# First product of the expert layer: float32r pairs become float16 pairs, and local heads are loaded in runs of six tokens

## The chip, the cores and the metric

The kernel runs on one core of a Trainium2 chip. The metric is the device time of one launch in microseconds (us). The kernel before took 700.45 us, the median of three runs (696.98 to 703.68). The engines are named as in the profile: PE (matrix products), PEld (PE's weight loads), DVE and ACT (vector and scalar engine), POOL (GpSimd) and SP, whose queue issues every DMA.

## The reference

Three layers follow each other. There are 4 batches of 576 tokens, 8 heads of 64 columns, and 2304 tokens of 512 columns in all.

```python
scores = q @ k.T / 8;  mask: heads 0-3 local (0 <= i-j < 32), heads 4-7 strided (j <= i, i % 32 == j % 32)
attn = softmax(where(mask, scores, -1e9));  x = attn @ v          # laid out as 2304 x 512
h = x @ w_in                                                      # 512 x 1024, the "first product"
sm = softmax(h);  solu = h * sm
ln = (solu - mean) / sqrt(var + 1e-6) * g_ln;  x = ln @ w_out     # 1024 x 512
a = x @ w_a;  b = x @ w_b;  out = (a * b) @ w_out2                # 512 x 1536 twice, 1536 x 512
```

q, k and v are float32; the weights arrive as float64 and are turned into float32 on the chip.

## The kernel before

**Order.** Every piece of work is recorded with `P.op` (engine, function, what it reads and writes); `Plan.schedule` (L243) then emits the pieces in the order of the list of numbers `ISSUE`. Each engine runs its own instructions strictly in that order, and the SP queue issues its DMAs in it too. Semaphores for the data and for the reuse of buffers follow from it.

**Attention.** A batch has four groups of two heads, two strided and then two local. `load_qk` (L549) loads q and k of a group; a strided group takes one DMA each, a local one takes a DMA per head and tensor, with 96 tokens on the partitions and runs of one token (64 floats). PE transposes them (L608), ACT copies the result out (L615, L618). Per tile, PE makes masked scores (L696, L701); DVE takes the row maximum (L719), subtracts it (L728), sums (L732) and inverts; ACT does the exponential (L731); POOL multiplies by the inverse (L768 or L777). Then there are two ways. A *direct* group (all of batch 0) is transposed in float32 by PE (L764), copied by ACT (L774) and multiplied with raw v in float32 (L798). Any other group is split: ACT writes a float16 copy of the weights (L784), POOL the rest (L785), the SP queue transposes the pair by DMA (L786), and v is a scaled float16 pair too (L644 on ACT, L647 on DVE), so that PE runs three float16 products (L803 to L805). The scale of v comes from `pair_scale` (L624), one for each two groups: a DVE maximum per group (L630), and a chain of small steps between PE and DVE (`pow2_scale`, L500 to L516). ACT writes the result to `xT` (L825).

**First layer.** `moe1` works on 18 tiles of 128 tokens. ACT rounds `xT` to float32r (`xh`, L845), DVE makes the rest (`xl`, L849). PE adds three passes (xh by the high weights, xh by the low weights, xl by the high weights), each of 4 products of 512 columns for each half of `h`, 24 in all (L856). `h` has one buffer: the next tile's products wait until DVE has taken the row maximum (L861), POOL has made a factor of it (L867 to L869) and DVE has multiplied `h` with the exponential (L871). ACT and DVE then make a float16 pair of the centred result (L875, L876), a DMA transposes it, and PE multiplies it with `w_out` in 48 products of 256 columns for each tile (L910).

**Weights of the first product.** `load_win` (L482) handles eight blocks of 128 x 512: SP loads the float64 words, ACT (L455) and DVE (L461, L465) make float32, ACT rounds to float32r (L474) and POOL subtracts (L475). A block's high half is ready as soon as it has been converted. `w_out` follows in the same way, but as a float16 pair with one scale for all (L492, L524, L526).

**Second layer.** From about 288 us on, float16 products of 384 and 256 columns (L1326, L1472) fill PE to the end.

## Time and profile before

| | |
|---|---|
| median of 3 runs | 700.45 us (696.98 to 703.68) |
| the profiled execution | 695.03 us, its span 693.3 us |
| busy: PE, DVE, ACT, POOL | 664.4, 571.5, 447.2, 144.7 us |
| idle of PE within the span | 28.9 us |

The profiled execution has 1.73 us around its span, and lies 5.42 us under the median. Engine rows count an instruction from its start to its end; neighbours on one engine overlap a little, so that a sum of means is some per cent above the busy time. A window of the profile gives the busy time of each engine in a stretch, and the rows of the timeline give the start of each instruction in us from the start of the span.

### The profile page before, as it was taken

The numbers are of one execution on the slowest core, as the hardware profiler recorded it, in microseconds if no ns is written. First come the engines' busy times: TensorE is split into PE (matmuls) and PEld (weight loads), VectorE is DVE, ScalarE is ACT, GpSimd is POOL, SyncE is SP. The second block draws the span as 40 slices with busy tenths as digits, with TensorE's granted clock in tenths as the row PEclk, the third lists the DMA queues.
The fourth block names the chain that finished last, engine by engine and source line by source line (L and its number), as shares of the span: only waits on it lengthen the run. The fifth ranks groups of instructions, "written<-read, shape, count | busy, mean of one in ns | idle before, by whom it ended". The sixth has DMA issues, their size and how long they took to land.

```text
span 693.3 us, 15572 instructions
## 1 busy us (share of the span) xinstructions
PE 664.4 (96%) x5991; PEld 498.8 (72%) x5991; DVE 571.5 (82%) x1238; ACT 447.2 (65%) x898; POOL 144.7 (21%) x268
## 2 busy tenths in 40 slices
PE   5987899999999999999999999999999999999997
PEld 4766677878787888886576676766767676775676
DVE  5789899789678644999999999799977989786576
ACT  3679868777767644986978787676543746434421
POOL 5544546536537432410000000000000000000000
PEclk9999899999999999999999999999999999999999
DMA  9999979999998434677254043653522304641023
GB/s 209 258 243 244 188 138 194 264 186 268 222 248 199 102 81 102 188 249 240 103 184 152 0 141 104 198 201 97 175 100 94 120 32 166 237 138 46 1 92 122
DMA packets 152650, 109.68 MB, mean 158 GB/s; under 512 B 101376, under 2 KB 131072, under 8 KB 152576
## 3 DMA queue, kind: packets, MB, share of 16 engines
q1 hardware_dynamic: 152576, 108.69, 60.4%
q8 instruction: 47, 0.77, 0.5%
q14 instruction: 27, 0.22, 0.1%
HBM read 65.41 MB, written 27.53 MB: 134 GB/s over the span
## 4 chain that ended last, share of the span: by engine, by line
PE 61%; DVE 8%; ACT 5%; issue 1%; POOL 0%; ACTq 0%; POOLq 0%
PE N L1326 17%; PE M L1326 13%; PE N L1472 9%; PE y L910 7%; PE M L1472 7%; PE h L856 6%; ACT y L1267 1%; DVE p L1423 1%; ACT w L1128 1%; DVE w L1132 1%; DVE y L1269 1%; DVE A L1415 1%; DVE A L1393 1%; DVE V L647 0%; ACT Z L1238 0%
## 5 line engine op out<-in xcount | busy, mean ns | idle before, releaser
L1326 PEld LDWEIGHTS <-w 128*128 128x128 f16 x1512 | 147.9, 98 | 91.7 <-issue 2.0
L1326 PE MATMUL N<-y,w 128*128 128x384 f16 x864 | 156.2, 326 | 0.7 <-ACT N L1333 0.7
L1472 PEld LDWEIGHTS <-p 128*128 128x128 f16 x1071 | 104.7, 98 | 20.4 <-issue 1.1
L1326 PE MATMUL M<-y,w 128*128 128x384 f16 x648 | 118.5, 326 | 0.8 <-ACT N L1333 0.8
L910 PE MATMUL y<-lnT,wout 128*128 128x256 f16 x864 | 101.4, 273 | 1.5 <-DMA lnT<-ln 0.8
L910 PEld LDWEIGHTS <-wout 128*128 128x128 f16 x864 | 82.0, 98 | 15.2 <-issue 4.1
L1418 ACT CAST p<-A 128x384 f16<-128x384 f32 x119 | 59.2, 512 | 40.1 <-DVE A L1393 22.6
L856 PE MATMUL h<-win,xh 128*128 128x512 f32 x288 | 79.8, 417 | 2.7 <-DVE wk L871 2.6
L1472 PE MATMUL N<-wo,p 128*128 128x256 f16 x612 | 77.7, 273 | 1.0 <-DVE yst L1488 1.0
L856 PEld LDWEIGHTS h<-win,xh 128*128 128x128 f32 x288 | 54.4, 198 | 14.4 <-DVE wk L871 3.3
L1423 DVE TENSOR_TENSOR p<-A,p 128x384 f16<-128x384 f32 x119 | 62.3, 552 | 2.7 <-ACT p L1418 2.7
L1472 PE MATMUL M<-wo,p 128*128 128x256 f16 x459 | 60.2, 273 | 0.0
L455 ACT ACTIVATE f64f<-raw 128x512 f32<-128x512 f32 x52 | 34.6, 674 | 11.2 <-DMA raw<-in_moe_w_in_dram 7.3
L856 PE MATMUL h<-win,xl 128*128 128x512 f32 x144 | 39.2, 394 | 0.0
L1415 DVE TENSOR_TENSOR A<-A 128x384 f32<-128x384 f32 x72 | 39.0, 553 | 0.2
L1488 DVE SCALAR_TENSOR_TENSOR ob<-M,osc,ob 128x256 f32<-128x256 f32 x63 | 27.8, 477 | 12.6 <-PE M L1472 11.1
L777 POOL TENSOR_TENSOR e<-e,r 128x324 f32<-128x324 f32 (+2 forms) x30 | 26.2, 881 | 50.0 <-DVE r L738 28.2
L861 DVE TENSOR_REDUCE st<-h 128x1 f32<-128x1024 f32 x18 | 22.0, 1220 | 17.2 <-PE h L856 17.1
L856 PEld LDWEIGHTS h<-win,xl 128*128 128x128 f32 x144 | 26.7, 188 | 5.9
L465 DVE SCALAR_TENSOR_TENSOR f64f<-f64f,raw 128x512 int32<-128x512 int32 x36 | 28.8, 804 | 2.3 <-ACT f64f L455 1.8
L1348 ACT COPY V<-M 128x384 f32<-128x384 f32 x36 | 17.0, 473 | 20.0 <-PE M L1326 19.9
L871 DVE SCALAR_TENSOR_TENSOR wk<-h,st,wk 128x1024 f32<-128x1024 f32 x18 | 23.0, 1279 | 7.8 <-POOL st L869 7.7
(191 smaller groups left out, 1207.0 us busy)
## 6 DMA issues: line engine op xcount, KB each, us to landing
raw<-in_moe_w_out_dram SPq DMA_DIRECT2D x20, 512.0 KB
o_scr<-ob SPq DMA_DIRECT2D x36, 256.0 KB
ob<-o_scr SPq DMA_DIRECT2D x30, 256.0 KB
raw<-in_moe_w_a_dram SPq DMA_DIRECT2D x12, 512.0 KB
raw<-in_moe_w_b_dram SPq DMA_DIRECT2D x12, 512.0 KB
y_scr<-y SPq DMA_DIRECT2D x14, 384.0 KB
y<-y_scr SPq DMA_DIRECT2D x14, 384.0 KB
y_scr<-ys SPq DMA_DIRECT2D x18, 256.0 KB
```

What stands on the lines that cost most here:

```text
L455: act(0.67, lambda: nc.scalar.activation(f(), raw()[:, :, 1].bitcast(F32), AF.Prelu, scale=2.0 ** -112, alpha=-2.0 ** 32), (raw,), (f,))
L465: dve(0.77, lambda: nc.vector.scalar_tensor_tensor(g().bitcast(I32), f().bitcast(I32), 3, raw()[:, :, 0], op0=ALU.logical_shift_left, op1= ...
L777: pool(0.1 + 1.2 * pl, lambda: nc.gpsimd.tensor_tensor(ev(), ev(), r()[:, :ng].unsqueeze(2).to_broadcast([128, ng, nk]), op=ALU.mult), (r, ...
L856: nc.tensor.matmul(h()[:, 512 * n:512 * n + 512], xs[xa]()[:, kk], win[wa][:, kk, 512 * n:512 * n + 512], start=(pi == 0 and kk == 0), sto ...
L871: dve(1.3, lambda: nc.vector.scalar_tensor_tensor(e(), h(), st()[:, 7:8], e(), op0=ALU.mult, op1=ALU.mult, accum_out=st()[:, 2:3]), (h, (s ...
L910: nc.tensor.matmul(y()[:, 256 * mi:256 * mi + 256], wout[:, kk, wa, 128 * m:128 * m + 128], lnT()[:, xa, kk], start=(pi == 0 and kk == 0), ...
L1326: nc.tensor.matmul(to()[:, :HB], w()[:, wa, a, kk], y7[b]()[:, xa, kk], start=first and pi == 0 and kk == 0, stop=pi == 2 and kk == 1, ski ...
L1415: dve(TD, lambda: nc.vector.tensor_tensor(to(), x(), y(), op=op), toks, (to,))
L1418: act(0.5, lambda: nc.scalar.copy(pu(0, a), x()), (x,), (pu.tok(0, a),))
L1423: dve(TD, lambda: nc.vector.tensor_tensor(pu(1, a), x(), pu(0, a), op=ALU.subtract), (x, pu.tok(0, a)), (pu.tok(1, a),))
L1472: nc.tensor.matmul(bk(i), pus[u](xa, a)[:, 128 * tt:128 * tt + 128], wo()[:, u, b, wa], start=a == A11 and u == 0 and pi == 0, stop=u == U ...
L1488: dve(0.475, lambda: nc.vector.scalar_tensor_tensor(dst(), bk(i), s(), dst(), op0=ALU.mult, op1=ALU.add), (src, osc), (obt(t, c),))
```

## The change

Four things change together.

1. `w_in` becomes a float16 pair. The eight blocks are converted to float32 (without rounding), ACT takes a sum of absolute values of each (L482 of the new file), one scale is made for all eight (`scale_win`), and only then are the pairs written: the high half by ACT (L489), the low half by DVE (L491, before on POOL). `xh` and `xl` are float16. The row maximum gets a small multiplication on DVE (L895), and POOL one more on its factor (L905), since `h` is now scaled.
2. v has one scale for each batch instead of each pair of groups (`batch_scale`), also in batch 0. `xT` stays scaled, and `unscale` holds the factor that takes both scales back.
3. The local groups of batch 0 are no longer direct: they are split like those of the later batches.
4. q and k of a local group come in one DMA each, with six neighbouring tokens on a partition (runs of 384 floats); POOL brings them into the former layout (L607).

```diff
-PARAM = dict(back=12, first=40, early=(0,), seed=4, noise=0.1, direct=((0, 0), (0, 1)), stay=0.0, pf1=(),
+PARAM = dict(back=12, first=40, early=(0,), seed=4, noise=0.1, direct=((0, 0),), stay=0.0, pf1=(),
-             PT=3, raw=2, rawl=2, raws=2, qkT=2, V=2, wk=2, xt=1, ln=2, lnT=2, ys=2, raw64=3, f64f=4, att=100.0,
+             PT=3, rawx=2, raw=2, rawl=4, raws=2, qkT=2, V=2, wk=2, xt=1, ln=2, lnT=2, ys=2, raw64=3, f64f=4, att=100.0,
...
 ISSUE = [int(n) for n in """
-10 0 13 11 14 5 2 15 16 1 12 6 18 17 21 8 35 19 9 20 7 4 22 414 37 430 3 771 787 36 39 38 40 43 41 42 181 187 23 66 44
...
-    win = [winp.tile([128, 4, FF1], F32R, name=f"win{i}") for i in range(2)]
+    win = winp.tile([128, 9, 2, DM], F16, name="win")
...
-        ring("win", tag, [128, 4, 128], F32R, pm["xt"])
+        ring("win", tag, [128, 4, 128], F16, pm["xt"])
...
-        split(f, lambda: win[0][:, kk, w], lambda: win[1][:, kk, w], ("win", kk, n), ph=i in pm["ph1"])
+        f = from_f64(w_in[128 * kk:128 * kk + 128, 1024 * n:1024 * n + 1024], False, fo, (("wif", c),))
+        act(0.78, lambda: nc.scalar.activation(f(), fo, AF.Abs, accum_out=wim[:, c:c + 1]), (("wif", c),), (f, ("wim", c)))
+    def scale_win():
+        pow2_scale(lambda: wim, [("wim", c) for c in range(8)], 8, 2, lambda: wisc, "wisc")
+    def split_win(c):
+        fo = win_f32(c)
+        act(0.71, lambda: nc.scalar.activation(win[:, c, 0], fo, AF.Copy, scale=wisc[:, 0:1]),
+            (("wif", c), "wisc"), (("wif", c - 1), ("win", c, 0)))
+        dve(0.85, lambda: nc.vector.scalar_tensor_tensor(win[:, c, 1], fo, wisc[:, 0:1], win[:, c, 0],
+                                                         op0=ALU.mult, op1=ALU.subtract),
+            (("wif", c), "wisc", ("win", c, 0)), (("wif", c - 1), ("win", c, 1)))
...
-            for h in range(2):
-                dma(lambda t=t, h=h, src=src: nc.sync.dma_start(
-                    out=tokens(t)[:, :, h], in_=src[h].rearrange("(m p) d -> p m d", p=QT)), (), ((t, h),), 190000)
+            src = src.rearrange("h (p m) d -> p h (m d)", p=QT)
+            dma(lambda t=t, src=src: nc.sync.dma_start(out=t().rearrange("p (h n) -> p h n", h=2), in_=src),
+                (), ((t, 0), (t, 1)), 225000)
...
+            if not g.strided:
+                flat, raw = raw, rings["rawx"].new()
+                pool(0.95, lambda flat=flat, raw=raw: nc.gpsimd.tensor_scalar(
+                    raw().rearrange("p (m h d) -> p m h d", m=NM, h=2), flat().rearrange("p (h m d) -> p m h d", h=2, m=NM),
+                    1.0, 1.0, op0=ALU.mult, op1=ALU.mult), ((flat, 0), (flat, 1)), ((raw, 0), (raw, 1)))
...
-    def pair_scale(gs):
+    def batch_scale(gs):
...
+            if is_direct(g):
+                junk = rings["V0"].new()
+                act(0.3 + n * 0.95e-3, lambda g=g, i=i, rows=rows, n=n, junk=junk: nc.scalar.activation(
+                    junk().bitcast(BF16)[:rows, :n], g.rawv()[:rows, :n], AF.Abs, accum_out=am()[:rows, i:i + 1]),
+                    g.vtoks, (am, junk))
+                continue
...
+    def batch_unscale(b, sc):
+        pool(0.4, lambda: nc.gpsimd.tensor_tensor(unscale[:, b:b + 1], sc()[:, 1:2], wisc[:, 1:2], op=ALU.mult),
+             (sc, "wisc"), (("un", b),))
...
-            nc.scalar.activation(to, xf, AF.Copy, scale=1.0 if direct else g.sc()[:, 1:2])
+            nc.scalar.activation(to, xf, AF.Copy, scale=g.sc()[:, 0:1] if direct else 1.0 / PSCALE)
...
-        dve(1.22, lambda: nc.vector.tensor_reduce(st()[:, 0:1], h(), axis=AX.X, op=ALU.max, negate=True), (h,), ((st, 0),))
+            nc.vector.tensor_reduce(st()[:, 8:9], h(), axis=AX.X, op=ALU.max, negate=True)
+            nc.vector.tensor_tensor(st()[:, 0:1], st()[:, 8:9], un, op=ALU.mult)
...
+            nc.gpsimd.tensor_tensor(st()[:, 9:10], st()[:, 7:8], un, op=ALU.mult)
...
-        for p in (gs[:2], gs[2:]):
-            for g in p:
-                load_v(g)
-            if not is_direct(p[0]):
-                pair_scale(p)
+        for g in gs:
+            load_v(g)
+        scales.append(batch_scale(gs))
```

The list `ISSUE` is new from end to end, so the same kinds of work stand in another order. Three places matter below.

**SP, at the start.** Before, six loads of v (`raws`) and the loads of q and k stood ahead of the first float64 block of `w_in`:

```order
L556 DMA rawk<-in_k_dram 96x3x256
L570 DMA raws_111<-in_v_dram 18x5x128
L570 DMA raws_111<-in_v_dram 18x6x128
L570 DMA raws_111<-in_v_dram 18x5x128 x2
L570 DMA raws_111<-in_v_dram 18x6x128
L570 DMA raws_111<-in_v_dram 18x5x128
L560 DMA rawq<-in_q_dram 96x6x64 x2
L560 DMA rawk<-in_k_dram 96x6x64 x2
L454 DMA raw_252<-in_moe_w_in_dram 128x1024
```

Now three blocks of `w_in` stand between the first loads of q and k:

```order
L562 DMA rawq<-in_q_dram 96x3x256
L562 DMA rawk<-in_k_dram 96x3x256
L459 DMA raw_143<-in_moe_w_in_dram 128x1024
L562 DMA rawq<-in_q_dram 96x3x256
L459 DMA raw_151<-in_moe_w_in_dram 128x1024
L562 DMA rawk<-in_k_dram 96x3x256
L459 DMA raw_156<-in_moe_w_in_dram 128x1024
L576 DMA raws_113<-in_v_dram 18x6x128
```

What moved: the first three blocks of `w_in` are asked for third, fifth and seventh.

**DVE, ahead of the first row maximum of `h`.** Before (`sm`, `r` and `e` belong to attention, `raw` to a conversion, `am` to a scale of v):

```order
L465 SCALAR_TENSOR_TENSOR wout<-f64f,raw_619 128x512
L732 TENSOR_REDUCE sm_745<-e_114 128x2
L736 SCALAR_TENSOR_TENSOR sm_745<-sm_745,over 128x2
L738 RECIPROCAL r<-sm_745 128x2
L461 TENSOR_SCALAR raw_675<-raw_675 128x512
L465 SCALAR_TENSOR_TENSOR wout<-f64f,raw_675 128x512
L461 TENSOR_SCALAR raw_719<-raw_719 128x512
L630 TENSOR_REDUCE am<-raws_112 128x1
L465 SCALAR_TENSOR_TENSOR wout<-f64f,raw_719 128x512
L861 TENSOR_REDUCE st<-h 128x1
```

In the change, this is where the scale of `w_in` (`wisc`) is written and the low halves begin; the row maximum comes 35 rows after the first of them, and 40 rows later in the queue than before:

```order
L525 TENSOR_TENSOR wisc<-xbank,units 128x2
L767 RECIPROCAL r<-sm_706 128x4
L757 TENSOR_TENSOR e_116<-s,mx 128x192
L470 SCALAR_TENSOR_TENSOR wout<-f64f,raw_568 128x512
L491 SCALAR_TENSOR_TENSOR win<-win,wisc 128x512
L765 SCALAR_TENSOR_TENSOR sm_711<-sm_711,over 128x2
L466 TENSOR_SCALAR raw_589<-raw_589 128x512
L767 RECIPROCAL r<-sm_711 128x2
L761 TENSOR_REDUCE sm_755<-e_116 128x2
L470 SCALAR_TENSOR_TENSOR wout<-f64f,raw_589 128x512
L491 SCALAR_TENSOR_TENSOR win<-win,wisc 128x512
```

**PE, ahead of the first product.** Before, two of the six local tiles of batch 0 had been multiplied with v when the first `h` began, and a float32 transpose of another stood directly ahead of it:

```order
L798 MATMUL xbank<-PT,rawl 64x64 x8
L608 MATMUL s<-ident,rawq 128x12x8 x2
L608 MATMUL s<-ident,rawq 128x2x6x8 x2
L608 MATMUL s<-ident,rawq 128x12x8 x2
L764 MATMUL y<-ident,e_114 96x128 x4
L856 MATMUL h<-win_108,xh 128x512 x4
L856 MATMUL h<-win_109,xh 128x512 x4
```

Now three of them stand ahead of it, and the float16 products of the third directly so:

```order
L832 LDWEIGHTS V_608
L832 MATMUL xbank<-PT,V_608 64x64
L833 LDWEIGHTS V_608
L833 MATMUL xbank<-PT,V_608 64x64
L834 LDWEIGHTS V_631
L834 MATMUL xbank<-PT,V_631 64x64
L885 LDWEIGHTS xh
L885 MATMUL h<-win,xh 128x512
```

The transposed weights `PT` of these tiles now come by DMA, and a float16 product has its weight load as an instruction of its own.

## Rows read from the trace of the kernel before

**Rows 1.** Windows: stretch, its length, busy time and count of each engine, clock, DMA.

```profile
0.00:51.90 51.90, 40.27 (x452) 32.89 (x452) 37.42 (x89) 29.66 (x58) 26.14 (x46) 1.00 1.01 237
51.90:172.90 121.00, 111.78 (x1428) 88.99 (x1425) 109.40 (x228) 96.15 (x186) 63.50 (x109) 0.97 1.05 212
172.90:288.00 115.10, 113.64 (x1219) 93.84 (x1220) 76.85 (x157) 73.69 (x131) 48.80 (x105) 1.00 0.74 166
288.00:693.30 405.30, 398.73 (x2901) 283.10 (x2899) 347.83 (x769) 247.66 (x525) 6.26 (x10) 1.00 0.39 130
...
10.00:20.00 10.00, 6.88 (x82) 5.72 (x84) 5.92 (x16) 5.55 (x12) 2.70 (x3) 1.00 1.12 236
```

**Rows 2.** Waits of PE before 52 us: for whom, us, times, longest.

```profile
PE s L608 <- DMA rawq<-in_q_dram: 4.2, 1, 4.2
```

**Rows 3.** Timelines: the first, ninth and last row maximum of `h` on DVE.

```profile
51.89 1.22 DVE L861 TENSOR_REDUCE st<-h 128x1 f32<-128x1024 f32 x1
172.91 1.22 DVE L861 TENSOR_REDUCE st<-h 128x1 f32<-128x1024 f32 x1
287.96 1.22 DVE L861 TENSOR_REDUCE st<-h 128x1 f32<-128x1024 f32 x1
```

**Rows 4.** Groups of DVE by shape, to 310 us: busy us, mean ns, idle before.

```profile
L526 DVE SCALAR_TENSOR_TENSOR wout<-wout,gs_sb 128x512 f16<-128x512 f32 x8 | 5.9, 735 | 0.0
L647 DVE SCALAR_TENSOR_TENSOR V<-rawl,sc,V 96x1152 f16<-96x1152 f32 x6 | 9.0, 1506 | 1.5 <-ACT V L644 1.5
L630 DVE TENSOR_REDUCE am<-rawl 96x1 f32<-96x1152 f32 x6 | 8.0, 1334 | 1.0 <-DMA rawl<-in_v_dram 1.0
L728 DVE TENSOR_TENSOR e<-s,mx 128x324 f32<-128x324 f32 x16 | 7.4, 484 | 0.0
L465 DVE SCALAR_TENSOR_TENSOR wout<-f64f,raw 128x512 int32<-128x512 int32 x8 | 5.5, 686 | 0.6 <-ACT f64f L455 0.5
L461 DVE TENSOR_SCALAR raw<-raw 128x512 int32<-128x512 int32 x29 | 16.1, 557 | 3.7 <-DMA raw<-in_moe_w_in_dram 3.7
L738 DVE RECIPROCAL r<-sm 128x4 f32<-128x4 f32 x16 | 2.7, 169 | 0.1
```

**Rows 5.** Timelines: a conversion on DVE and POOL's subtraction beside it.

```profile
25.90 1.81 DVE L465 SCALAR_TENSOR_TENSOR f64f<-f64f,raw 128x512 int32<-128x512 int32 x1
25.90 1.27 POOL L475 TENSOR_TENSOR win<-f64f,win 128x512 fp32r<-128x512 f32 x1 [2.33 <-ACT win L474]
```

**Rows 6.** The chain that ended last, PE at full pace: start, us, line, count.

```profile
266.00 5.26 PE y L910 x48
271.25 5.47 PE h L856 x24
...
465.46 3.90 PE N L1326 x24
```

**Rows 7.** Timelines of DVE and PE late in the layer: one turn of `h`.

```profile
254.48 1.22 DVE L861 TENSOR_REDUCE st<-h 128x1 f32<-128x1024 f32 x1 [2.81 <-PE h L856]
257.46 1.28 DVE L871 SCALAR_TENSOR_TENSOR wk<-h,st,wk 128x1024 f32<-128x1024 f32 x1 [1.16 <-POOL st L869]
259.45 2.09 PE L856 MATMUL h<-win,xh 128*128 128x512 f32 x8
```

**Rows 8.** Timelines: transposes on SP, and the product that waited for them.

```profile
151.06 2.57 SPq L786 DMA_TRANSPOSE PT<-P  x2
161.66 0.20 PE L803 MATMUL xbank<-PT,V 54*64 54x54 f16 x2
```

**Rows 9.** Timeline of PE: start, us; the first eight products of `h`.

```profile
43.80 3.52 PE L856 MATMUL h<-win,xh 128*128 128x512 f32 x8
```

**Rows 10.** Groups of PE by shape, to 310 us: busy us, mean ns, idle before.

```profile
L764 PE MATMUL y<-ident,e 128*96 128x128 f32 x20 | 4.7, 368 | 0.7 <-ACT PT L774 0.7
L798 PE MATMUL xbank<-PT,rawl 96*64 96x64 f32 x72 | 4.3, 271 | 2.9 <-ACT PT L774 2.9
L803 PE MATMUL xbank<-PT,V 96*64 96x64 f16 x108 | 7.6, 203 | 0.0
```

More of the change, by code (lines that the diff above doesn't have):

```diff
@@ L354, in tile_banded_attention_solu_bilinear @@
     wsc = const.tile([128, 2], F32, name="wsc")
+    wim = const.tile([128, 8], F32, name="wim")
+    wisc = const.tile([128, 2], F32, name="wisc")
+    unscale = const.tile([128, B + 2], F32, name="unscale")
     small = const.tile([128, 78], F32, name="small")
@@ L387, in tile_banded_attention_solu_bilinear @@
     ring("conv", "f64f", [128, 512], F32, pm["f64f"])
-    for tag, n in (("am", 2), ("m1", 1), ("sc", 2), ("row", 2), ("mx", 6), ("sm4", 6), ("r", 6)):
+    for tag, n in (("am", 4), ("m1", 1), ("sc", 2), ("row", 2), ("mx", 6), ("sm4", 6), ("r", 6)):
         ring("sm", tag, [128, n], F32, 6 if n == 6 else 4)
-    ring("wk", "st", [128, 8], F32, 4)
+    ring("wk", "st", [128, 10], F32, 4)
     ring("psR", "s", [128, 2, 512], F32, 2)
@@ L617, in evac @@
                 else:
-                    nc.scalar.activation(dst.rearrange("p (i t) -> p i t", i=2), src, AF.Copy, scale=sc)
+                    nc.scalar.activation(dst.rearrange("p (w i o) -> p w i o", i=2, o=NM // 2),
+                                         src.rearrange("p i (o w) -> p w i o", w=QT), AF.Copy, scale=sc)
             act(0.65, evac, (tp,), ((g.T, c),))
@@ L963, in load_next @@
             loaded[0] += 1
+    scales = []
     def attention(b):
@@ L991, in tile_banded_attention_solu_bilinear @@
         load_win(i)
+    P.key = pm["win"] + 0.1
+    scale_win()
+    batch_unscale(0, scales[0])
+    for i in range(8):
+        split_win(i)
     P.key = pm["wout"] - 1
```

50 lines of the change are left out of this document (28 added, 22 removed), and 264 rows, old and new, of the table ISSUE.

## The prediction

> **What bounds the kernel now.** Read the windows first [rows 1]. From 288 us to the end PE is busy 398.73 of 405.30 us, and from 172.9 to 288 us it is busy 113.64 of 115.10: there PE's own work sets the time. Before, it does not. From 51.9 to 172.9 us PE idles 9.2 us and DVE 11.6, so both are near their limit; to 51.9 us PE idles 11.6 us and DVE 14.5. Of PE's idle time only 4.2 us is the wait for the first load [rows 2]; the rest is in-order work that waits for other engines. Then read where the row maxima of `h` stand [rows 3]: the first at 51.89, the ninth at 172.91, the last at 287.96 us. They are the marks by which I follow the change: the start decides the first, DVE's queue the next eight, PE's queue the rest. Behind the last one nothing is touched, and I take its 405.3 us as they are.
>
> The profiled execution took 695.03 us, 5.42 under the median of 700.45. I work out a difference against the profiled one and add it to the median, taking it that executions differ evenly.
>
> **To the first row maximum.** I count DVE's queue ahead of it in both orders. The change has there 8 low halves of `w_in`, 2 of v, 1 more maximum of v (net), 9 more passes of strided attention, 5 more conversion steps and 16 more small instructions. Prices [rows 4]: a low half of `w_in` is the same instruction on the same size as one of `w_out`, 8 x 0.735 = 5.9; 2 x 1.506 = 3.0; 1.3; 9 x 0.484 = 4.4; two conversions at 0.686 and three shifts at 0.557, 3.0; 16 at 0.169, 2.7. Sum 20.3 us. About 13 of them are new work and the rest is later work brought forward. The queue's 37.42 us thus become 57.7.
>
> DVE's idle time there was 14.5 us. Some 4.1 of it lie between 10 and 20 us [rows 1], where DVE waited for data, and the change asks for three blocks of `w_in` right at the start; the larger runs of the local loads help in the same direction. The two scale chains add short waits of DVE for PE, but other DVE work stands between their steps. I take 10 us of idle time, so the first row maximum comes at 57.7 + 10 = 67.7, say 67 us. The lower bound is 62: 5 us of idle time at the least, since DVE has nothing to do until the first loads have landed at 4.2 us [rows 2]. The upper bound is 72, with all 14.5. This does not ask how fast the first product runs: its eight first products took 3.52 us, against 2.09 for eight later on [rows 9, 7], PE being at the lower of its two levels (1.2 and 2.4 GHz) though the granted clock reads 1.00 [rows 1], and I leave that as it is.
>
> What is moved for nothing: ACT gets eight sums of absolute values, but has 22 idle us in the stretch [rows 1]. POOL loses its eight subtractions at 1.27 and gets copies of the local q and k and six subtractions in their place. The subtractions were also a burden to DVE: a conversion beside one took 1.81 us instead of 0.69 [rows 5, 4]. I count no gain from that, since POOL's new work takes their place. The Trainium skill, GPSIMD Engine Reference, section Specifications, says that POOL shares its way to SBUF with VectorE, and that instructions of VectorE with two SBUF inputs contend. This row agrees; by the rule eight conversions at a gain of up to 1.1 us would bring the first mark to about 59, and the time to about 697.
>
> **From the first to the ninth.** What came forward is missing here: 9 attention passes of 324 columns (4.4 us), one low half of v (1.5), a conversion (1.2), four shorter passes (1.6) and 23 small steps (3.9), against two more maxima of v (2.3) and eight small multiplications behind the row maximum (1.4): 8.9 us less by [rows 4]. Means overlap a little, so I take 8. With the idle time of before the 121.0 us become 113, and the ninth row maximum stands at 67 + 113 = 180, 7.1 us later than before.
>
> **From the ninth to the last.** Here PE sets the pace. Back to back, 24 products of `h` take 5.47 us, 228 ns each; 48 of 256 columns take 5.26 (110 ns) and 24 of 384 columns 3.90 (162.5 ns), both float16 [rows 6]. On the line through these, 512 columns in float16 take 215.4 ns. That saves 12.5 ns a product: 2.7 us on the 216 from the ninth mark on, 5.4 on all 432. The weight loads become instructions of their own, but behind 215 ns they are as hidden as those behind the 110 ns of `y` are. So the last mark is 7.1 - 2.7 = 4.4 us late.
>
> The longer turn of `h`: between the row maximum and the end of the multiplication lie 4.26 us (254.48 to 258.74), and PE takes `h` up at 259.45 [rows 7], 0.7 later. The change adds a small DVE step and a POOL step, 0.2 to 0.6 us together (a small step is 0.169 on DVE [rows 4]). It is covered by the 48 products of `y` up to 0.7; I count 0.4 in all. The ends are 0 and 2 us, for five turns.
>
> **Sum:** +4.8 us, which is 705.2 against the median, 0.7% slower.
>
> The loads of local q and k (half as many DMAs) I cost at nothing beyond the start, as PE's waits for loads are that one of 4.2 us; if the queues were what held DVE back, the gain would show in the first stretch, and the lower bound has it. The six new DMA transposes on SP are a matter for a rival.
>
> **Rivals.** *A, the start is hidden:* DVE has 26.1 us of idle time before the ninth mark, and if 13 of it can be squeezed out, PE's work alone counts. Then the kernel gains 5.4 us on `h` and, on batch 0, the float32 transposes and products (4.7 + 4.3 us) less a third of what the float16 products of three batches take, (7.6 x 3) / 3 = 7.6 [rows 10]: 1.4. Where `h` is mixed with other work eight products took 2.09 us from the first start to the last end [rows 7], at most 261 ns each, and not having this is worth another 1 to 2. Together 8 us: 692.5. For it speaks that DVE's idle time is large; against it, that the queue is in order and the scale needs the last block of all eight, where before a block's high half was ready by itself.
>
> *B, the transposes come late:* the first product now stands on PE directly behind the third local tile's float16 products, and these wait for a DMA transpose, where PE and ACT did it before. Two transposes issued from 151.06 on were still awaited at 161.66 [rows 8], 10.6 us later, and the start is a time of full queues too (DMA share 1.01). The Trainium skill, VectorE: DVE Perf Modes, section The three transpose paths, gives 390 ns for 128 x 128 on TensorE and 1309 ns by DMA. By that rule, an estimate, a tile of eight blocks takes 10.5 us by DMA if they go one after another; the row is not far from it. In this rival DVE keeps all of its 14.5 us of idle time, waiting for `h`: the first mark comes at 72.2, 5.2 us later than I forecast, and the time is 710.4. It is over the bound of 1% when the first mark comes later than 69.
>
> *C, the pairs are not faster:* if the float16 product still takes 228 ns, as when the extra weight load instructions are not hidden, 5.4 us are missing (2.7 of the sum, and what A would have had). The time would be 708 to 710.
>
> **Chances.** The forecast 0.42, A 0.24, B 0.27, C 0.07. About 1% (7 us) is what a measurement of this kernel can tell from no change. Faster by more than that: most of A, 0.17. Slower: B, C and the upper end of the forecast (idle time of 12.5 or more), 0.36. Within 1%: 0.47. The forecast's own range is 700 to 708: a first mark at 62 to 70. The range of 8 in 10 has to reach to A and to B: 691 to 713.
>
> **What would show it.** The first row maximum at 62 to 72 us, the ninth at 175 to 185, and from there to the last 112 to 114 us. 24 products of `h` back to back in 5.2 us. DVE's idle time ahead of the first mark near 10 us; PE's waits before it for the weights of the third local tile (B) or for `xh` and the low halves of `w_in`. I am wrong if the ninth mark is no later than before (then DVE did not set that stage), or if the stretch behind the last mark is no longer 405 us.

## The result, and the profile after

The changed kernel took 704.47 us (median of 11 runs, 702.74 to 706.41), the kernel before 701.76 in 11 runs (694.55 to 703.68). The ratio, which counts the fast runs alone, is 1.0075, with a 95% interval of 1.0049 to 1.0100. That is 5 us slower, inside the 1% that was forecast as no change. The two medians lie only 2.7 us apart; in the later rounds the kernel before had medians of 699.33 to 699.96 us (51 runs), 4.5 to 5.1 under 704.47. The forecast was 705.2 us.

The windows of the changed kernel, cut at its own first, ninth and last row maximum (columns as in [rows 1]), and two parts of the first stretch. The clock of 1.00 in the three rows that begin before 65 us is not a measurement throughout: the trace has no record of the granted clock before 65.0 us (last section).

```profile
0.00:72.30 72.30, 46.66 (x618) 34.05 (x618) 54.39 (x129) 48.12 (x100) 32.34 (x56) 1.00 0.98 219
72.30:185.62 113.32, 102.96 (x1272) 67.30 (x1273) 103.02 (x197) 89.18 (x168) 68.46 (x121) 0.95 1.09 224
185.62:296.54 110.92, 110.62 (x1227) 75.87 (x1228) 78.36 (x168) 72.40 (x129) 57.75 (x121) 1.00 0.70 155
296.54:702.70 406.16, 398.43 (x2890) 281.80 (x2887) 347.50 (x770) 247.94 (x525) 6.57 (x12) 1.00 0.39 130
20.00:50.00 30.00, 18.14 (x222) 13.42 (x221) 20.10 (x48) 20.09 (x42) 9.06 (x9) 1.00 1.08 235
50.00:72.30 22.30, 17.73 (x256) 12.05 (x256) 21.79 (x50) 19.40 (x42) 13.01 (x15) 1.00 0.94 201
```

The start has become 20.4 us longer than in [rows 1], the stretch to the ninth mark 7.7 shorter, the one to the last mark 4.1 shorter, and behind it 0.9 is added: +9.4 us in all between the two profiles. The ratio shows less, because the first profile of the kernel before was one of its shortest executions; a second one (below) is closer to its median. DVE's 54.39 busy us of the start leave 17.9 idle, 9.9 of them between 20 and 50 us. From 50 us to the first mark it is busy 21.79 of 22.30 us.

The three marks on DVE's timeline (start, duration), as in [rows 3]:

```profile
72.30 1.22 DVE L894 TENSOR_REDUCE st<-h 128x1 f32<-128x1024 f32 x1
...
185.62 1.20 DVE L894 TENSOR_REDUCE st<-h 128x1 f32<-128x1024 f32 x1
...
296.54 1.22 DVE L894 TENSOR_REDUCE st<-h 128x1 f32<-128x1024 f32 x1
```

What DVE waited for ahead of the first mark (us, times, longest):

```profile
DVE raw L466 <- DMA raw<-in_moe_w_in_dram: 4.4, 4, 3.2
DVE am L648 <- DMA rawl<-in_v_dram: 3.5, 2, 2.0
DVE sm L761 <- ACT e L760: 2.9, 3, 2.5
DVE m L510 <- PE xbank L827: 1.5, 1, 1.5
DVE m L515 <- PE xbank L514: 1.1, 1, 1.1
...
DVE m L515 <- PE xbank L827: 0.9, 1, 0.9
...
DVE m L510 <- PE xbank L509: 0.5, 1, 0.5
```

Two kinds of wait in this list are new at the start. The one scale of v for the whole batch needs the local v (`am` on `rawl`, 3.5 us), and the two scale chains stand on DVE until PE has done its part (the four rows of `m` on `xbank`, 4.0 us).

The chain that ended last, late in the layer, answers to [rows 6]: 24 products of `h` take 5.19 us instead of 5.47.

```profile
273.54 5.24 PE y L946 x48
278.77 5.19 PE h L885 x24
```

A late turn of `h`, as in [rows 7], on DVE and on PE:

```profile
250.56 1.23 DVE L894 TENSOR_REDUCE st<-h 128x1 f32<-128x1024 f32 x1 [2.14 <-PE h L885]
...
254.41 1.28 DVE L907 SCALAR_TENSOR_TENSOR wk<-h,st,wk 128x1024 f32<-128x1024 f32 x1
```

```profile
251.64 4.54 PE L946 MATMUL y<-lnT,wout 128*128 128x256 f16 x40
256.01 1.89 PE L885 MATMUL h<-win,xh 128*128 128x512 f16 x8
```

From the row maximum to PE's next `h` it is 5.45 us here, 4.97 before; 40 products of `y` fill PE meanwhile, and PE does not stand still.

### The profile page after: what moved, and what is told of

Its sections match the earlier page's. It is cut to its first block, busy times and chain, and to the rows that moved or that the text cites. A ratio compares the mean times of both kernels' runs of the same rounds, so it can differ in the third digit from the quotient of the medians.

```text
span 702.7 us, 15656 instructions
## 1 busy us (share of the span) xinstructions
PE 658.7 (94%) x6003; PEld 459.0 (65%) x6003; DVE 583.3 (83%) x1260; ACT 457.6 (65%) x919; POOL 165.1 (23%) x309
## 4 chain that ended last, share of the span: by engine, by line
PE 68%; DVE 5%; ACT 3%; issue 1%; POOL 0%; DVEq 0%; ACTq 0%
PE N L1369 18%; PE M L1369 13%; PE N L1515 10%; PE y L946 8%; PE h L885 8%; PE M L1515 7%; ACT y L1310 1%; DVE y L1312 1%; PE s L619 1%; PE xbank L832 1%; DVE w L1175 1%; PE s L730 1%; DVE p L1466 0%; DVE A L1436 0%; DVE yst L1320 0%
## 5 line engine op out<-in xcount | busy, mean ns | idle before, releaser
L1369 PE MATMUL M<-y,w 128*128 128x384 f16 x648 | 120.3, 326 | 2.7 <-ACT N L1376 2.6
L885 PE MATMUL h<-win,xh 128*128 128x512 f16 x288 | 73.7, 396 | 4.6 <-DVE wk L907 3.8
L885 PEld LDWEIGHTS <-xh 128*128 128x128 f16 x288 | 28.0, 101 | 36.0 <-issue 9.0
L806 POOL TENSOR_TENSOR e<-e,r 128x384 f32<-128x384 f32 (+2 forms) x36 | 32.7, 913 | 32.9 <-DVE r L767 21.6
L885 PE MATMUL h<-win,xl 128*128 128x512 f16 x144 | 37.5, 383 | 0.0
L814 POOL TENSOR_TENSOR P<-e,P 128x384 f16<-128x384 f32 (+2 forms) x36 | 30.9, 865 | 10.9 <-ACT P L813 10.7
L912 DVE SCALAR_TENSOR_TENSOR ln<-wk,st,ln 128x1024 f16<-128x1024 f32 x18 | 23.7, 1317 | 8.0 <-ACT ln L911 7.9
L1531 DVE SCALAR_TENSOR_TENSOR ob<-N,osc,ob 128x256 f32<-128x256 f32 x45 | 20.2, 477 | 9.0 <-PE N L1515 9.0
## 6 DMA issues: line engine op xcount, KB each, us to landing
rawq<-in_q_dram SPq DMA_DIRECT2D x16, 288.0 KB
```

Source lines behind the costliest of these rows:

```text
L806: pool(0.1 + 1.2 * pl, lambda: nc.gpsimd.tensor_tensor(ev(), ev(), r()[:, :ng].unsqueeze(2).to_broadcast([128, ng, nk]), op=ALU.mult), (r, ...
L814: pool(0.15 + 1.4 * pl, lambda: nc.gpsimd.tensor_tensor(plo, ev(), ph, op=ALU.subtract), (e, ("P2", pi, 0)), (("P2", pi, 1),))
L885: nc.tensor.matmul(h()[:, 512 * n:512 * n + 512], xs[xa]()[:, kk], win[:, 4 * n + kk, wa], start=(pi == 0 and kk == 0), stop=(pi == 2 and ...
L912: dve(1.3, lambda: nc.vector.scalar_tensor_tensor(ln()[:, 1], e(), st()[:, 3:4], ln()[:, 0], op0=ALU.add, op1=ALU.subtract), (e, (st, 3), ...
L1369: nc.tensor.matmul(to()[:, :HB], w()[:, wa, a, kk], y7[b]()[:, xa, kk], start=first and pi == 0 and kk == 0, stop=pi == 2 and kk == 1, ski ...
L1531: dve(0.475, lambda: nc.vector.scalar_tensor_tensor(dst(), bk(i), s(), dst(), op0=ALU.mult, op1=ALU.add), (src, osc), (obt(t, c),))
```

## The experiments

The marks of every profile, in us; a number in brackets is the stretch that ends there. The ratio is that to the kernel before, with its 95% interval.

| kernel | first | ninth | last | ratio |
|---|---|---|---|---|
| before, first profile | 51.9 | 172.9 (121.0) | 288.0 (115.1) | |
| before, second profile | 52.6 | 176.2 (123.6) | 292.1 (115.9) | |
| changed | 72.3 | 185.6 (113.3) | 296.5 (110.9) | 1.0075 (1.0049 to 1.0100) |
| pairs alone, on before | 54.1 | 174.7 (120.6) | 287.3 (112.6) | 0.9953 (0.9922 to 0.9983) |
| pairs and loads, on before | 53.1 | 180.9 (127.8) | 294.4 (113.5) | 1.0033 (1.0010 to 1.0057) |
| low halves on POOL | 72.3 | 185.4 (113.1) | 296.3 (110.9) | 1.0093 (1.0059 to 1.0128) |
| no wait for the scale | 70.0 | 184.0 (114.1) | 296.3 (112.3) | 1.0049 (1.0026 to 1.0071) |
| low halves twice | 77.7 | 192.0 (114.3) | 302.9 (110.9) | 1.0188 (1.0146 to 1.0229) |
| local data first | 80.1 | 193.0 (112.8) | 303.9 (110.9) | 1.0183 (1.0151 to 1.0214) |
| local data first, no wait | 74.7 | 190.8 (116.2) | 301.7 (110.9) | 1.0145 (1.0114 to 1.0176) |
| loads as before | 71.0 | 185.6 (114.6) | 300.3 (114.7) | 1.0120 (1.0085 to 1.0156) |
| batch 0 local direct | 75.8 | 189.1 (113.3) | 300.0 (110.9) | 1.0117 (1.0084 to 1.0151) |
| `xl` twice | 73.2 | 191.1 (117.9) | 304.8 (113.7) | 1.0172 (1.0130 to 1.0214) |
| more products | 75.0 | 192.8 (117.8) | 310.6 (117.9) | 1.0256 (1.0207 to 1.0304) |

**The kernel before, a second profile.** Expected:

> The kernel before, unchanged, for a second profile: its executions so far lie between 694.6 and 704.5 us, and the first profile was one of the shortest (695.0). If an execution is longer because of how the loads at the start fall, the difference lies ahead of the first row maximum (51.9 us) or the ninth (172.9), and the stretch behind the last mark is again 405.3 us.

It took 699.41 us. Its windows, cut at its marks:

```profile
0.00:52.59 52.59, 40.01 (x456) 32.74 (x456) 36.38 (x88) 29.99 (x58) 26.46 (x46) 1.00 1.01 234
52.59:176.19 123.60, 113.95 (x1421) 90.46 (x1420) 109.68 (x228) 95.86 (x185) 63.67 (x109) 0.94 0.99 205
176.19:292.07 115.88, 113.74 (x1219) 93.68 (x1219) 76.52 (x156) 74.38 (x133) 48.98 (x105) 1.00 0.76 168
292.07:697.60 405.53, 398.92 (x2902) 283.11 (x2899) 347.72 (x769) 247.90 (x525) 6.30 (x10) 1.00 0.39 130
```

Of the 4.3 us between the two profiles, 2.6 lie between the first and the ninth mark. Against this one the changed kernel's ninth mark is 9.4 us late, its last 4.5 and its end 5.1, which is what the ratio says. Of the 2.6 us, 1.9 lie between the third and the fourth mark: 21.98 us in the first profile (76.79 to 98.77 us), 23.92 in the second (78.50 to 102.42). The granted clock reads 0.92 and 0.86 there, that is, PE was at its lower level for 3.4 and for 6.8 us, and the same 268 products keep it busy 19.08 and 20.31 us. So part of what makes executions differ is the clock; what made it stay down longer in one of them is not shown.

**Pairs alone, on the kernel before.** The operands of `h` become float16; there is no scale.

```diff
-    win = [winp.tile([128, 4, FF1], F32R, name=f"win{i}") for i in range(2)]
+    win = [winp.tile([128, 4, FF1], F16, name=f"win{i}") for i in range(2)]
...
-        ring("win", tag, [128, 4, 128], F32R, pm["xt"])
+        ring("win", tag, [128, 4, 128], F16, pm["xt"])
...
```

> The kernel before with one thing changed: the first product's operands are float16 pairs instead of float32r pairs, without any scale (the pair's low part then loses some bits); order, loads, attention and weights' handling stay. The forecast's theory (PE sets only the stretch from the ninth row maximum to the last, 216 products at 12.5 ns less): first and ninth row maximum where they were (52 and 173 us, within 1), from the ninth to the last 112.4 instead of 115.05, or 111 if the changed kernel's whole gain there (4.1 us) comes from the products; time 2.7 to 4.1 us under the kernel before, a ratio of 0.994 to 0.996. Rival A (the faster product counts from the start on): ninth row maximum 2 to 4 us earlier too and a time 5 to 7 us under the kernel before, 0.990 to 0.993. Rival C (pairs not faster): ratio 1.000, 24 products of h back to back again in 5.47 us.

It took 695.83 us, 0.9953 of the kernel before: the fastest of all here. Two of its windows and a row of its chain:

```profile
54.11:174.73 120.62, 110.72 (x1428) 73.77 (x1429) 109.58 (x228) 95.60 (x186) 63.36 (x109) 0.94 1.04 212
174.73:287.31 112.58, 109.46 (x1209) 74.63 (x1208) 76.54 (x157) 73.70 (x131) 48.89 (x105) 1.00 0.76 170
```

```profile
270.89 5.20 PE h L856 x24
```

From the ninth mark to the last it is 2.5 us shorter than the first profile of before and 3.3 shorter than the second. Its first mark is 1.5 to 2.2 us later than theirs, and its ninth, 174.7 us, lies between theirs (172.9 and 176.2). Whether something is gained up to there can't be read from that: from the first to the ninth mark it is 0.4 us shorter than the first profile, whose granted clock reads 0.97 there, and 3.0 shorter than the second, which reads 0.94 as this one does. The forecast's step holds, and rival C does not: the pairs are faster where PE is full. Rival A's ratio (0.990 to 0.993) reaches into the interval, so a gain ahead of the ninth mark is neither shown nor excluded.

**Low halves of `w_in` on POOL.**

```diff
-        dve(0.85, lambda: nc.vector.scalar_tensor_tensor(win[:, c, 1], fo, wisc[:, 0:1], win[:, c, 0],
-                                                         op0=ALU.mult, op1=ALU.subtract),
+        pool(1.4, lambda: nc.gpsimd.tensor_tensor(win[:, c, 1], fo, win[:, c, 0], op=ALU.subtract),
...
```

> The changed kernel, with the eight low halves of w_in made on POOL instead of DVE, in the same places of the order. For that POOL subtracts without a factor: the scale of w_in is still worked out in all its steps, but 1.0 is used. Theory D (DVE's queue sets the first and the ninth row maximum; the low halves are 7.5 us of it): the first row maximum comes at 65 to 67 instead of 72.3, the ninth at 178 to 179 instead of 185.6, and the time is about 7 us under the changed kernel's, 697 to 698 (0.994 of the kernel before). Rival P (POOL and DVE slow each other): the eight subtractions of 1.3 us stretch DVE's instructions beside them by 3 to 6 us, so the ninth row maximum is only 2 to 4 us earlier, 700 to 702. Rival S (the wait for the scale, ACT's late high halves and the third tile's transposes set the first product at 63.4 us): the first row maximum not before 70.5, the time 702 to 704.

706.35 us; the first mark stays at 72.28. DVE's busy time ahead of it fell by 1.5 us, not by 7.5. Groups of DVE by shape (busy us, mean ns, idle before), of this kernel between 48 and 72.3 us:

```profile
L472 DVE SCALAR_TENSOR_TENSOR wout<-f64f,raw 128x512 int32<-128x512 int32 x5 | 6.8, 1362 | 0.7 <-ACT f64f L462 0.6
...
L766 DVE SCALAR_TENSOR_TENSOR sm<-sm,over 128x2 f32<-128x2 f32 x2 | 2.2, 1113 | 0.0
```

and of the changed kernel between 50 and 72.3:

```profile
L491 DVE SCALAR_TENSOR_TENSOR win<-win,wisc 128x512 f16<-128x512 f32 x8 | 7.5, 935 | 0.1
L470 DVE SCALAR_TENSOR_TENSOR wout<-f64f,raw 128x512 int32<-128x512 int32 x5 | 4.4, 876 | 0.1
...
L765 DVE SCALAR_TENSOR_TENSOR sm<-sm,over 128x2 f32<-128x2 f32 x2 | 0.3, 148 | 0.0
```

With POOL subtracting, DVE's conversions take 1.36 instead of 0.88 us, and a step on two columns 1.11 instead of 0.15, as the conversion in [rows 5] did: six of the 7.5 us that DVE gives away come back as longer instructions, 4.3 of them in these two rows. Rival P's stretching is shown, at the upper end of its price (3 to 6 us). Its marks and its time are not: it had the ninth mark 2 to 4 us earlier and 700 to 702 us. For from 48 us on DVE is busy only 20.07 of 24.28 us here, and the first mark still does not move: DVE's queue alone does not hold it. Rival S had this mark (not before 70.5 us), though its time of 702 to 704 us was too low too. The Trainium skill, GPSIMD Engine Reference, section Specifications, says that POOL shares its SBUF interface with VectorE and that instructions with two SBUF inputs contend; the stretched rows here are of that kind.

**No wait for the scale.** The scale chain is worked out, but 1.0 is used, and the halves follow their own block.

```diff
-            (("wif", c), "wisc"), (("wif", c - 1), ("win", c, 0)))
+            (("wif", c), "small"), (("wif", c - 1), ("win", c, 0)))
...
```

> The changed kernel, in which no block of w_in waits for the scale: the steps of the scale chain stay where they are, but 1.0 is used, so each block's high and low half can follow its own conversion, and they are moved there (seven and sixteen places behind it in the order of all pieces, between 15 and 45 us instead of 52 to 70). No engine's work changes. Theory D+idle (DVE idles 17.9 us before the first row maximum, almost all of it before 50 us, and is full from 50 us on; the halves that wait for the scale cannot use that time): the 7.5 us of low halves and ACT's 5.8 us of high halves go into idle time, the first product starts at 56 to 60 instead of 63.4, the first row maximum comes at 65 to 67, the ninth at 178 to 180, the time is 697 to 699. Rival W (the idle time before 50 us is waiting for loads, and what is put in front of them only comes to wait too): first row maximum at 70 to 72, time within 1.5 us of the changed kernel.

702.94 us. The first mark is 2.3 us earlier; of that, 1.6 is left at the ninth and 0.2 at the last. DVE is no longer full ahead of the first mark:

```profile
50.00:69.97 19.97, 17.67 (x245) 12.01 (x244) 16.36 (x45) 15.12 (x34) 12.05 (x16) 1.00 1.13 226
```

The halves did go into idle time (16.36 busy of 19.97 us now), and the first product starts at 62.52 instead of 63.36. So neither DVE's full queue behind the scale nor the wait for the scale decides more than 2.3 us of the start. Rival W comes nearest (70 to 72 us). The intervals of this ratio and of the changed kernel's overlap, so that a gain in time is not shown.

**Low halves twice.** The same instruction, issued two times (`for _ in range(2)`).

> The changed kernel, with each of the eight low halves of w_in made twice over on DVE. Theory D (DVE full from 50 us to the first row maximum, and near its limit to the ninth): first row maximum 6.5 to 8 us later (79 to 80), ninth as much later (192 to 193.5), last 5 to 7.5 us later, time 710 to 712, a ratio of 1.012 to 1.015 to the kernel before. Rival S (other waits set the first product): ninth at most 2 us later, time 704.5 to 706.5.

712.98 us. DVE's busy time ahead of the first mark rises from 54.39 to 60.00:

```profile
0.00:77.70 77.70, 47.85 (x618) 34.34 (x618) 60.00 (x138) 48.41 (x100) 33.19 (x56) 0.74 0.87 205
```

The first mark is 5.4 us later (theory D had 6.5 to 8), the ninth and the last 6.4, and rival S is excluded. Work added where DVE is full passes through nearly whole. Making room there, in the two runs above, gave back 0.0 and 2.3 us.

**Batch 0's local groups direct again.** `direct=((0, 0), (0, 1))`, with the replaced steps in their places of the order.

> The changed kernel with the local groups of batch 0 direct again, as before: float32 transposes on PE and raw v in place of pairs and DMA transposes, in the places of the order where the replaced steps stood. DVE loses two low halves of v (2.75 us) and two maxima of v (2.7 us; ACT sums absolute values instead), POOL six subtractions, SP six DMA transposes; PE gets 20 float32 transposes and float32 products. Theory D (DVE's queue sets the first mark): first row maximum at 67 to 69, ninth at 180 to 182, time 699 to 701. Theory B (the transposes by DMA come late): first row maximum at 66 to 69 too, but with DVE's idle time lower by 3 to 5 us besides. Rival S (the start is a chain of loads and of PE at its lower level; DVE's 5.4 us were in its idle time): first row maximum 71 to 74, time 703 to 706.

708.30 us. DVE does 6.6 us less ahead of the first mark, and that is 3.5 us later:

```profile
0.00:75.83 75.83, 52.60 (x606) 37.78 (x606) 47.82 (x126) 49.33 (x103) 25.19 (x49) 0.73 0.81 196
```

```profile
DVE m L511 <- PE xbank L828: 2.9, 1, 2.9
DVE m L516 <- PE xbank L515: 2.8, 1, 2.8
DVE m L511 <- PE xbank L510: 2.6, 1, 2.6
DVE m L516 <- PE xbank L828: 2.4, 1, 2.4
```

The second fence lists DVE's waits in the scale chains: 10.7 us, against 4.0 in the changed kernel, because PE now has 5.9 us more to do among the chains' steps. The forecasts of theories D and B both fail here. But the run takes 6.6 us from DVE and gives 5.9 to PE at once, so it does not show what less work on DVE alone would do.

**Local data first, and both together.** Order alone: q and k of the second local group and the local v ahead of the fourth and fifth block of `w_in`; then the same on the kernel without the wait for the scale.

> The changed kernel in another order of its loads: q and k of the second local group of batch 0 (their transposes began at 22.3 and 25.6 us before and begin at 30.9 and 35.0 us in the changed kernel) and the two local v are asked for ahead of the fourth and fifth block of w_in, whose conversions move back with them. No work is added or taken away. Theory L (the start is set by when batch 0's local data land; the blocks of w_in put in front of them cost the start 9 us there): second local group's k transposed by 28 to 31 us, DVE's idle time before the first row maximum falls from 17.9 to 12 to 14 us, first row maximum at 66 to 69 instead of 72.3, ninth at 179 to 183, time 700 to 702. Rival F (the queues are full from 2 to 55 us, DMA share 0.94 to 1.12, so that what is put in front pushes back something else that is awaited as well): first row maximum 71 to 74, time within 1.5 us of the changed kernel's 704.5.

> The changed kernel with the order of loads of the run that puts batch 0's local data first, and the halves of w_in behind their own blocks as in the run without the wait for the scale (1.0 is used for the scale). If both waits are part of the same chain (first the late local data, then the halves that pile up behind the scale): first product on PE at 55 to 58 instead of 63.4, first row maximum at 62 to 66, ninth at 176 to 180, time 696 to 699. If the start is bound by the amount of work and data: no better than the better one of the two alone, first row maximum 68 to 71, time 701 to 703.

712.05 and 709.72 us, both slower than the changed kernel. Waits of the first of them, up to 80 us:

```profile
DVE raw L467 <- DMA raw<-in_moe_w_in_dram: 9.0, 5, 3.1
...
ACT V L645 <- DMA raws<-in_v_dram: 7.4, 1, 7.4
...
PE y L794 <- ACT PT L804: 6.8, 1, 6.8
```

The strided v, now later, held ACT for 7.4 us, PE waited for ACT, and the second local group's transposes began at 35.2 and 39.2 us although its data had been asked for sooner. Rival F came nearest for the first run, but it had 71 to 74 us and 1.5 us at most where 80.1 and 7.6 were measured; the second run, with its first product at 67.6 us and its first mark at 74.7, was later than both of its forecasts. The runs settle nothing on when the data must land: in an order made for five queues together, a change to one of them can cost more than it brings.

**Loads as before.** Two DMAs per tensor in runs of one token. POOL's copy is kept but copies straight, and ACT copies the transposed q and k out in the former layout.

```diff
-            src = src.rearrange("h (p m) d -> p h (m d)", p=QT)
...
+                    nc.sync.dma_start(out=t().rearrange("p (m h d) -> p m h d", m=NM, h=2)[:, :, h],
+                                      in_=src[h].rearrange("(m p) d -> p m d", p=QT))
...
```

> The changed kernel with the local q and k loaded as before: two DMAs for each tensor, in runs of one token (64 floats), in the former layout; POOL's copy stays, but copies straight. The prediction's reason (the loads' pattern costs and gives nothing beyond the start): first row maximum within 1.5 us of 72.3, time within 1.5 us of the changed kernel. Rival R (runs of 256 bytes take the queues longer than runs of 1536, and the queues are full to 55 us): local q and k land 1 to 3 us later for each group, first row maximum 74 to 77, ninth as much later, time 706 to 709.

708.20 us, 3.7 over the changed kernel, but not at the start, which is 1.3 shorter. The loss lies behind the ninth mark:

```profile
185.64:300.29 114.65, 112.43 (x1227) 76.91 (x1228) 79.25 (x168) 72.49 (x129) 57.67 (x121) 0.99 0.74 150
```

PE idles 2.2 us there instead of 0.3, and its own work is 1.8 longer. One row of its timeline holds most of the idle time, a wait for the copy of transposed q and k:

```profile
216.89 0.56 PE L732 MATMUL s<-qkT 64*64 64x96 f32 x16 [1.97 <-ACT qkT L632]
```

In the windows around it the granted clock is 0.89 (212 to 220 us) and 0.87 (220 to 226), where the changed kernel reads 1.00 in both. From 218.2 to 221.6 us it reads 0.50: PE was at its lower level for 3.4 us, beginning 1.3 us after the end of that wait. What PE does there would have taken half as long at the upper level; that is an estimate, and it accounts for 1.7 of the 1.8 us. Here the rival named the right sign (later by 2 to 4 us) and the wrong place.

**Pairs and loads, on the kernel before.** The pairs, and the local loads in runs of six tokens with POOL's copies; each tensor still takes two DMAs, where the changed kernel has one.

> The kernel before with float16 pairs without a scale for the first product (the run that did this alone was at 0.9953 of the kernel before) and also with the local q and k loaded in runs of six tokens, brought into the former layout by a copy on POOL six places ahead of the transposes in the order. If the pattern of the loads is worth what its removal from the changed kernel cost (3.7 us, behind the ninth row maximum): 692 to 694, a ratio of 0.988 to 0.992, and the best of all kernels here. If POOL's 16 copies of 0.83 us hold up POOL's and DVE's other work as much as the loads give: 695 to 698, a ratio of 0.994 to 0.998.

701.66 us: the gain is gone. The stretch to the ninth mark is 127.8 us, 7.2 more than with the pairs alone. 5.9 of that lie between the seventh and the eighth mark (144.97 and 166.37 us). There PE waits for POOL's copy, and later POOL stands still for 8.7 us waiting for DVE (a row of PE's waits, and one of POOL's timeline with the idle time before it in brackets):

```profile
PE s L616 <- POOL rawx L604: 2.5, 1, 2.5
...
163.85 1.72 POOL L786 TENSOR_TENSOR e<-e,r 128x384 f32<-128x384 f32 x1 [8.66 <-DVE r L747]
```

PE's wait comes first. It ends at 149.87 us; from 150.1 to 160.3 us the granted clock reads 0.50, and PE is busy throughout. Between the two marks PE is thus busy 18.89 us, where the pairs alone need 14.91 for about as many products (229 and 233), and idle 2.5 us instead of 0.6: that is the 5.9 us. POOL's copy had stood in its queue behind the factor of the row maximum until 148.99 us. So in this profile PE's wait for the copy, and the lower clock that followed it, account for 5.9 of the 7.2 us. The loads' pattern is not worth 3.7 us by itself; what it gives or costs hangs on the order around it.

**Which engine sets the middle stretch.** Two doses on the changed kernel: DVE's `xl` made twice, and four more products per tile.

```diff
-            for d, c in cols:
+            for d, c in cols * 2:
```

```diff
+                    for kk in range(4 if n == 0 and pi == 0 else 0):
+                        nc.tensor.matmul(h()[:, 512 * n:512 * n + 512], xs[xa]()[:, kk], win[:, 4 * n + kk, wa],
+                                         start=kk == 0, stop=kk == 3)
```

> The changed kernel with xl (DVE's low half of a tile's input, 0.69 us) made twice over for each of the 18 tiles: 8 tiles lie between the first and the ninth row maximum, 9 between the ninth and the last. The forecast's claim (DVE sets the stretch from the first to the ninth, PE the one to the last): first to ninth 118 to 119 instead of 113.3 us, ninth to last 110.9 to 112, time 5.5 to 8 us over the changed kernel's 704.5. Rival G (from the first to the ninth both engines idle 10 us, and neither alone sets it; waits between them do): first to ninth 114 to 116, time 1 to 4 us over.

> The changed kernel with four more products of 512 columns for each tile of the first product (the first pass of its first half is run twice, the first time for nothing), 0.86 us each time: 6.9 us in the 8 tiles from the first to the ninth row maximum, 7.8 us in the 9 to the last. The forecast's claim (DVE sets the first stretch, PE the second): first to ninth 113 to 115.5, ninth to last 118 to 119 instead of 110.9, time 8 to 11 us over the changed kernel's. Rival P (PE sets both): first to ninth 119 to 120.5, time 15 to 17 over. Rival G (waits between the engines): first to ninth 115.5 to 118, time 11 to 14 over.

711.99 and 718.35 us. Windows from the first mark on, of `xl` twice:

```profile
73.21:191.13 117.92, 103.98 (x1272) 68.05 (x1273) 108.20 (x205) 88.89 (x168) 71.34 (x121) 0.94 1.05 221
191.13:304.78 113.65, 111.60 (x1228) 75.60 (x1229) 85.67 (x178) 72.43 (x129) 60.92 (x121) 1.00 0.67 145
```

and of the added products:

```profile
74.97:192.77 117.80, 109.58 (x1313) 69.83 (x1313) 102.03 (x197) 89.83 (x168) 67.59 (x121) 0.96 1.06 215
192.77:310.63 117.86, 117.86 (x1280) 79.11 (x1277) 78.27 (x168) 72.31 (x129) 57.46 (x121) 1.00 0.65 144
```

Between the first and the ninth mark, 5.2 us more of DVE's work cost 4.6, and 6.6 us more of PE's cost 4.5: both engines set that stretch by turns. In time the dose on DVE came out as the forecast's claim had it (7.5 us over), the dose on PE as rival G had it (13.9). Between the ninth and the last, PE's 7.2 us cost 6.9, and DVE's 7.3 cost 2.7: there it is PE, with a part of DVE's step on the way of each tile.

## Why the prediction was right, and where not

The total was right in good part by luck: its terms were off in both directions, and the errors cancelled. Against the second profile of before, which lies near the median, the start became 19.7 us longer (15.1 forecast), the stretch to the ninth mark 10.3 shorter (8 forecast), the one to the last mark 5.0 shorter (2.7 forecast), and 0.6 was added behind it: +5.1, where the forecast had +4.8. Against the first profile, from which the forecast was worked out, the ninth mark is 12.7 us late (7.1 forecast) and the last 8.6 (4.4 forecast). Of the signs that the forecast named, the first mark (72.3 for 62 to 72), the ninth (185.6 for 175 to 185), the stretch to the last (110.9 for 112 to 114) and DVE's idle time (17.9 for near 10) came out outside, and the 24 products (5.19 for 5.2) as said.

- **The first mark failed.** 67 us was forecast, 72.30 measured, at the upper bound of 72. DVE's queue was counted about right in sum (57.7 forecast, 54.39 measured; neighbours overlap), though a low half of `w_in` took 0.935 us and not 0.735. The step that failed is "I take 10 us of idle time": it was 17.9. It leaned on earlier loads and on other work between the steps of the scale chains. DVE's wait for the blocks of `w_in` did not get shorter: 4.4 us, against 3.7 in this row of the kernel before up to its first mark.

```profile
DVE raw L461 <- DMA raw<-in_moe_w_in_dram: 3.7, 3, 2.9
```

  The chains' waits for PE came to 4.0 us, and the new wait for the local v to 3.5. Nor is the mark DVE's queue plus a remainder, as the sum had it: with the low halves out of the full stretch it came only 2.3 us earlier, with them on POOL and DVE idle for 4.2 us behind 48 us not at all, and with 6.6 us less on DVE, but 5.9 more on PE, later.
- **Rival B** had the number (72.2 us) without the mechanism. From 50 us to the first product at 63.36, PE's waits are these, none of them for a transpose by DMA:

```profile
PE s L730 <- ACT qkT L626: 1.5, 1, 1.5
PE xbank L832 <- ACT xT L854: 1.3, 1, 1.3
PE xbank L524 <- DVE row L522: 1.0, 1, 1.0
...
```

  The two left out are 0.4 and 0.2 us, for ACT and PE itself. With the DMA transposes of batch 0 put back to PE the start became longer. The Trainium skill, VectorE: DVE Perf Modes, section The three transpose paths, gives PE's transpose as the shorter one; no run here shows when one by DMA lands, and the run shows only that the shorter path stood in a queue that others waited for.
- **First to ninth:** 113 forecast, 113.3 measured. That is 7.7 us less than in the first profile of before and 10.3 less than in the second. The number was DVE's 8 us; the doses show that PE's work counts as well, and PE had 8.8 busy us less there too [rows 1]. Half of the mechanism was missing, so that the agreement is in part luck.
- **Ninth to last:** 2.7 us forecast, 2.5 to 3.3 with the pairs alone; this step is shown. The weight loads are hidden, as the forecast had it; but they are no addition, for the trace of before has one for each product too, of 0.19 to 0.20 us, and in the changed kernel they take 0.10. In the changed kernel the stretch is 4.1 to 5.0 us shorter. PE's busy time fell by 3.0 us [rows 1]; the rest is its idle time, 1.5 before and 0.3 now, a matter of order and loads (with the loads as before it is 2.2). The longer turn of `h` is there, 5.45 instead of 4.97 us in one turn, but PE has work meanwhile, and the 0.4 us of the sum do not show.
- **Behind the last mark** 405.3 was taken; it is 406.2, and within 0.2 of that in most kernels with the changed order: 0.6 to 0.9 us that the sum lacks. The forecast had named a stretch other than 405 us as a sign of being wrong; where this comes from is not shown.
- **POOL's subtractions.** That no gain was counted for taking them off POOL was right: the changed kernel with them there was not faster. The reason was another one in part: with the low halves on POOL, DVE's longer instructions take back what DVE gives away.

What stays open is which chain of waits holds the start at 72 us. No part that was undone or moved by itself gave back more than 2.3 of its 20 us; undoing all but the pairs gave back 18. The forecast's 13 us of new work on DVE do not explain it by themselves: DVE was given room in three runs, and the mark came 2.3 us earlier, not at all, and (with more work on PE) later. Three rivals were not tested by themselves: the one scale of v for a whole batch, whose wait for the local v is 3.5 us; the new order of the list as such; and PE's own pace, since PE ran at its lower level until 65.0 us here and until 46.9 us before (last section).

## What to carry to other kernels

Where five in-order queues start up together, the busy sum of one engine plus a share of idle time is no forecast of a mark: count the new waits too (each step of a scale chain that crosses to another engine is one), and take the upper bound of the idle time unless a row shows what would shorten it. Try the cheap core of a change alone: here the pairs alone, with no scale, no new loads and no split of batch 0, gave 0.9953, and the whole change 1.0075. Where a difference of 5 us is to be read from profiles, take two of the kernel before: the first one here lay 6.7 us under the median of 11 runs, the second 2.3, and most of what parts them lies in the stretches that the change alters.

## What the runs showed of the hardware

- Twice PE stood still for 2 to 2.5 us in a stretch where it was otherwise busy, and the granted clock then fell to its lower level: after a wait of 1.97 us that ended at 216.89 us it reads 0.50 from 218.2 to 221.6 us (loads as before), and after one of 2.50 us that ended at 149.87 us it reads 0.50 from 150.1 to 160.3 us (pairs and loads). PE's busy time grew by 1.8 and by 4.0 us, beside 1.97 and 2.50 us of waiting. No run here takes the wait alone away.
- A DVE step on 128 x 2 elements, 0.15 us by itself, took 1.11 us beside a subtraction of POOL, and a conversion 1.36 instead of 0.88. With the low halves on POOL two such steps begin at 51.05 and 53.63 us, 0.5 us into a subtraction, and end with it: at 52.16 and 54.75 us, where POOL's end at 52.14 and 54.72.
- In the start PE ran at its lower level for most of the time, in the kernel before and in the changed one, although the window reads 1.00. The trace records changes of the granted clock, and a window ahead of the first record reads 1.00. In the changed kernel the first record is a rise at 65.0 us, in the kernel before one at 46.9 us. Six transposes of one size show the level ahead of it and behind it: in the changed kernel they take 1.19 to 1.22 us each time from 4.31 us on, and 0.66 us behind the rise.

```profile
61.42 1.22 PE L619 MATMUL s<-ident,rawk 96*128 96x96 f32 x6 [0.37 <-ACT qkT L626]
...
70.52 0.66 PE L619 MATMUL s<-ident,rawx 96*128 96x96 f32 x6
```

  With the low halves on POOL, where the records begin earlier and the clock reads 0.50 from 27.4 to 64.9 us, six such transposes take as long within that stretch, and 0.66 us behind it, at 70.46 us:

```profile
55.58 1.22 PE L620 MATMUL s<-ident,rawq 96*128 96x96 f32 x6
```

  That is why three profiles (low halves on POOL, low halves twice, local direct) read 0.73 to 0.74 in the first stretch and the changed kernel 1.00, while PE's busy time there hardly differs (47.18 and 47.85 us in the first two, against 46.66). The first eight products of `h` fit in: 3.43 us with the low halves on POOL, nearly all of them ahead of the rise; 2.70 us in the changed kernel, where they begin at 63.36 us and the rise comes 1.7 us later; 1.89 us late in the layer. The prediction was right that the eight of the kernel before (3.52 us from 43.80 us on [rows 9]) ran at the lower level.
